# Conversion with four load tiles, three tiles for scale and low part, and a chunk begun two places after its load

## The chip, the cores and the metric

The kernel runs on one core of one Trainium2 chip. The metric is the time of one execution on the device in microseconds (us); the median of several executions is compared. The engines are TensorE (PE in the profile, its weight loads PEld), VectorE (DVE), ScalarE (ACT), GpSimd (POOL) and SyncE (SP), which here issues nearly all transfers. Each engine works through its own instructions in order.

## The reference

Two stages follow one another. The first is attention with heads mixed twice (8 batches, 12 heads, 448 tokens, 64 numbers per head), all in float32:

```
scores = scale * q @ k^T;  scores = einsum('bhij,hg->bgij', scores, w_pre)
attn = softmax(scores);    attn   = einsum('bhij,hg->bgij', attn, w_post)
attn_out = attn @ v
```

The second takes the result as 3584 tokens of 768 numbers:

```
h = x @ w_in;  g = h - tanh(h);  out = g @ w_out     # w_in 768 x 2048, w_out 2048 x 768
```

`w_in` and `w_out` arrive as float64, that is as pairs of 32-bit words. The kernel makes two float32r numbers of each, a high and a low part, whose sum carries the precision that the products need. This step is the conversion.

## The kernel before, in words

**The attention stage** goes through 180 places (`NPL`), the passes of the loop `for p in range(NPL + 3)`. A place handles two groups of 10 tokens with all 12 heads: `premix` (L521, TensorE mixes the heads of the scores `t`), `expo` (L530 maximum on DVE, L532 exponential on ACT), and for the place before `norm` (L541, L542 on DVE, L543 `wr` on POOL) and `mix` (L560 on TensorE, with `e` and `wr`), whose result ACT copies at the start of the next place (`at`, L570 or L577). Between them a place gets jobs by a planner: scores (L477, copies L482), preparation of k and q (L417, L443), values (L602, copy L620). TensorE's order in a place is premix, jobs, mix. A place is therefore short (about 3.8 us) with scores alone and longer (5 to 6 us) with values. The tile that `mix` writes exists once, so the next mix waits for the copy `at`.

**Gathers.** Each place first issues on SP two gathers `t<-s` (L510), for the premix two places later. Then `issue` sends up to 6 waiting transfers, first those of the attention (`queue`), then those of the conversion (`slow`), in order, and only those that were entered in an earlier place.

**The conversion** works in 56 chunks, 24 of `w_in` (128 x 512 numbers, the wide ones) and 32 of `w_out` (128 x 384, the narrow ones), in the order 6 wide, 8 narrow, and so on. `narrow_chunk` is a generator of eleven steps: L80 (DVE) makes `cm` from the load tile `cr`; L82 (ACT) and L83 (DVE); L85 (ACT); L87 (DVE) writes `cs`; L89 and L94 (DVE); L96 and L98 (POOL) make the sum in `cm`; L102 (ACT) writes the high part into `cs`; L104 (POOL) writes the low part into `cl`; the last step enters the transfers of `cs` and `cl` to DRAM. `narrow_steps` keeps up to two chunks active and lets them step in turn. It enters a load when a load tile is free, and begins a chunk when its load was issued at least one place earlier (`landed(1)`); that is a count of places and no wait. The wait for the data itself stands on DVE, at L80. When no chunk is active, a step passes with nothing done.

`Steps` spreads these steps evenly: from place 4 on, `conv.place()` runs 617/164 = 3.76 steps at the end of every place, after the mix was written down. At place 177 `conv.rest(now)` runs what is left; between its steps `now` issues all waiting transfers. Directly after that the first weights (`load_w(0)`, `w<-ws`) and the inputs of the second stage (`load_x`, `rx<-xs`) are issued on SP.

At the end `in_order` fixes the order of instructions on every engine as they were written down. A conversion step that has to wait therefore holds up what is written behind it on its engine: on POOL the next `wr`, on ACT the next `at`, on DVE the next `zs` and maximum.

**The second stage** computes h, the gate and the sum for 7 blocks of 512 tokens, with 16 slices of the weights each.

Of the kernel before, what the change touches and what calls it, by code (L numbers as in the profile page):

```python
# [11 lines left out]
F32R = mybir.dt.float32r  # L12
I32 = mybir.dt.int32
# [8 lines left out]
def raw(ap):  # L22

    return ap.bitcast(F32)
# [7 lines left out]
CW = 512  # L32
# [5 lines left out]
def narrow_steps(nc, pool, dma, chunks):  # L38

    def load(src):
        p, n2 = src.shape
        r = pool.tile([p, CW, 2], I32, name="cr", tag="cr", bufs=3)[:, : n2 // 2]
        return r, dma(r.rearrange("p n t -> p (n t)"), src)


    todo, loads, active = list(chunks), [], []  # L50
    yield
    while todo or loads or active:
        while todo and len(loads) + len(active) < 3:
            src, dst = todo.pop(0)
            loads.append((*load(src), dst))
        while loads and len(active) < 2:
            r, landed, dst = loads[0]
            if not landed(1):
                break
            loads.pop(0)  # L60
            active.append(narrow_chunk(nc, pool, dma, r, dst))
        for it in list(active):
            if next(it, "end") == "end":
                active.remove(it)
            else:
                yield
        if not active:
            yield


def narrow_chunk(nc, pool, dma, r, dst):
    p, n, _ = r.shape
    hi, lo = r[:, :, 1], r[:, :, 0]
    m = pool.tile([p, CW], F32, name="cm", tag="cm", bufs=2)[:, :n]
    s = pool.tile([p, CW], I32, name="cs", tag="cs", bufs=2)[:, :n]
    u, w = hi, lo


    lim = 122879.9921875
    nc.vector.tensor_scalar(m, hi.bitcast(F32), lim, -lim, op0=ALU.min, op1=ALU.max)  # L80
    yield "step"
    nc.scalar.mul(m, m, 2.0**-112)  # L82
    nc.vector.tensor_scalar(w, lo, 8, None, op0=ALU.logical_shift_right)  # L83
    yield "step"
    nc.scalar.mul(w.bitcast(F32), w, 2.0**-44)  # L85
    yield "step"
    nc.vector.tensor_scalar(s, hi, -(2**31), None, op0=ALU.bitwise_and)  # L87
    yield "step"
    nc.vector.scalar_tensor_tensor(  # L89
        out=u, in0=m.bitcast(I32), scalar=3, in1=s, op0=ALU.logical_shift_left, op1=ALU.bitwise_or  # L90
    )
    yield "step"

    nc.vector.tensor_scalar(s, u, -(2**23), None, op0=ALU.bitwise_and)  # L94
    yield "step"
    nc.gpsimd.tensor_tensor(out=m, in0=w.bitcast(F32), in1=s.bitcast(F32), op=ALU.mult)  # L96
    yield "step"
    nc.gpsimd.tensor_tensor(out=m, in0=m, in1=u.bitcast(F32), op=ALU.add)  # L98
    yield "step"
    fh = s.bitcast(F32R)  # L100
    fl = pool.tile([p, CW], F32R, name="cl", tag="cl", bufs=2)[:, :n]
    nc.scalar.copy(fh, m)  # L102
    yield "step"
    nc.gpsimd.tensor_sub(fl, m, raw(fh))  # L104
    yield "step"
    for to, part in zip(dst, (fh, fl)):
        if len(to.shape) == 3:
            part = part.rearrange("p (f n) -> p f n", f=to.shape[1])
        dma(to, raw(part))
    yield "step"  # L110
# [38 lines left out]
def kernel_body(  # L149
# [189 lines left out]
    with ExitStack() as st:  # L339
# [403 lines left out]
        scores_of(1, 0)  # L743
        NPL = NG // 2
        conv = Steps(narrow_steps(nc, cv, partial(dma, to=slow), chunks), 11 * len(chunks) + 1, NPL - 16)


# [200 lines left out]
```

## Time and profile before

| | us |
|---|---|
| median of 3 runs | 1794.49 (1794.04 to 1794.81) |
| the profiled execution | 1788.92 |
| its span, first to last instruction | 1787.2 |
| TensorE busy | 1751.0 |
| VectorE busy | 1128.3 |
| ScalarE busy | 1000.5 |
| GpSimd busy | 320.1 |

Busy times are sums over one engine's instructions and overlap between engines. The time that counts is the chain of work that ends last; idle time of an engine beside that chain costs nothing.

### The profile page before, as it was taken

How to read it: one execution, taken by the hardware profiler on the slowest of the kernel's cores; microseconds unless marked ns; L12 is line 12 of the kernel's file. 1: busy time of each engine (PE TensorE's matmuls, PEld its weight loads, DVE VectorE, ACT ScalarE, POOL GpSimd, SP SyncE). 2: the span in 40 equal slices, each digit the busy share in tenths (PEclk: the TensorE clock that was granted, in tenths of full speed). 3: DMA queues.
4: the chain of work that ended last, by engine and by line, in shares of the span. 5: the costliest groups of instructions: out<-in, count | busy, mean ns of one | idle time of the engine just before them, and what ended most of it. 6: DMA issues, size and time to landing. Idle time of an engine off the chain costs nothing.

```text
span 1787.2 us, 41382 instructions
## 1 busy us (share of the span) xinstructions
PE 1751.0 (98%) x16572; PEld 1425.6 (80%) x16572; DVE 1128.3 (63%) x2362; ACT 1000.5 (56%) x2051; POOL 320.1 (18%) x417
## 2 busy tenths in 40 slices
PE   8999999999999999999999999999999999999998
PEld 6777777777777777777888888888888888888887
DVE  5676777777777767664556566565565565655555
ACT  5777877777777776765343443433434434444333
POOL 1333333333333333321010010000000000000000
PEclk9999999999999999999999999999999999999999
DMA  8668687777967687565655655655656655655651
GB/s 176 204 196 216 194 236 224 217 215 215 249 203 218 215 213 220 178 202 216 255 207 194 248 193 207 241 193 214 229 197 216 224 208 204 228 217 190 230 194 36
DMA packets 232816, 372.32 MB, mean 208 GB/s; under 512 B 98992, under 2 KB 207536, under 8 KB 218288
## 3 DMA queue, kind: packets, MB, share of 16 engines
q1 hardware_dynamic: 231740, 368.45, 64.0%
q8 instruction: 131, 2.15, 0.5%
q10 hardware_dynamic: 884, 1.22, 0.2%
q14 instruction: 61, 0.50, 0.1%
HBM read 245.37 MB, written 47.19 MB: 164 GB/s over the span
## 4 chain that ended last, share of the span: by engine, by line
PE 87%; DMA 4%; ACT 4%; DVE 3%; issue 1%; POOL 0%; SPq 0%; ACTq 0%; DVEq 0%; POOLq 0%
PE ps_o L560 13%; PE ps_h L257 8%; PE ps_h L258 8%; PE ps_h L262 8%; PE ps_m L602 8%; PE ps_p L521 7%; PE ya L305 6%; PE ya L302 6%; PE ya L303 6%; PE ps_q L477 5%; PE yb L305 3%; PE yb L303 3%; PE yb L302 3%; DMA t<-s 2%; PE ps_m L443 1%
## 5 line engine op out<-in xcount | busy, mean ns | idle before, releaser
L560 PEld LDWEIGHTS ps_o<-wr,e 60*112 60x112 f32 (+1 forms) x5760 | 306.2, 176 | 44.3 <-POOL wr L543 21.8
L560 PE MATMUL ps_o<-wr,e 60*112 60x60 f32 (+1 forms) x5760 | 315.5, 259 | 14.3 <-POOL wr L543 7.7
L530 DVE TENSOR_REDUCE mx<-ps_p 128x1 f32<-128x448 f32 x360 | 207.7, 619 | 163.9 <-PE ps_p L521 163.7
L532 ACT ACTIVATE e<-ps_p,mx 128x448 f32<-128x448 f32 x360 | 225.7, 634 | 101.9 <-DVE mx L530 99.4
L289 ACT CAST gh<-r 128x512 fp32r<-128x512 f32 x112 | 69.6, 621 | 372.6 <-DVE r L282 372.6
L258 PE MATMUL ps_h<-xl,w 128*128 128x512 f32 x672 | 264.4, 393 | 0.0
L257 PE MATMUL ps_h<-xh,w 128*128 128x512 f32 x672 | 264.3, 393 | 0.0
L570 ACT COPY at<-ps_o 112x960 f32<-112x960 f32 x156 | 153.7, 985 | 93.8 <-PE ps_o L560 93.2
L247 POOL TENSOR_TENSOR xl<-rx,xh 128x512 fp32r<-128x512 f32 x38 | 55.6, 1464 | 731.2 <-ACT xh L246 731.2
L521 PE MATMUL ps_p<-t,wpre 60*64 60x448 f32 (+1 forms) x1440 | 180.8, 569 | 3.9 <-DMA t<-s 2.7
L305 PE MATMUL ya<-w,gl 128*128 128x512 f32 x448 | 177.0, 395 | 0.7 <-DVE gl L290 0.7
L278 DVE SCALAR_TENSOR_TENSOR r<-qa,ps_h 128x512 f32<-128x512 f32 x112 | 77.1, 688 | 159.2 <-ACT t L275 159.2
L302 PE MATMUL ya<-w,gh 128*128 128x512 f32 x448 | 174.8, 390 | 1.0 <-ACT gh L289 1.0
L303 PE MATMUL ya<-w,gh 128*128 128x512 f32 x448 | 174.8, 390 | 0.0
L602 PEld LDWEIGHTS ps_m<-at,vr 112*64 112x64 f32 x3072 | 147.5, 137 | 31.0 <-ACT at L577 10.9
L262 PE MATMUL ps_h<-xh,w 128*128 128x512 f32 x672 | 170.6, 389 | 0.0
L602 PE MATMUL ps_m<-at,vr 112*64 112x120 f32 (+1 forms) x3072 | 161.6, 261 | 8.4 <-ACT at L577 3.1
L272 ACT ACTIVATE u<-ps_h 128x512 f32<-128x512 f32 x112 | 67.0, 599 | 152.9 <-PE ps_h L262 152.9
L262 PEld LDWEIGHTS ps_h<-xh,w 128*128 128x128 f32 x672 | 126.3, 188 | 26.3
L258 PEld LDWEIGHTS ps_h<-xl,w 128*128 128x128 f32 x672 | 127.5, 190 | 23.7
L257 PEld LDWEIGHTS ps_h<-xh,w 128*128 128x128 f32 x672 | 127.4, 190 | 23.4
L543 POOL TENSOR_TENSOR wr<-wpost,zs 128x120 f32<-128x120 f32 x180 | 70.2, 390 | 402.9 <-DVE zs L542 293.6
(93 smaller groups left out, 3038.0 us busy)
## 6 DMA issues: line engine op xcount, KB each, us to landing
w<-ws SPq DMA_DIRECT2D x112, 1536.0 KB
t<-s SPq DMA_DIRECT2D x342, 210.0 KB
cr<-in_moe_w_in_dram SPq DMA_DIRECT2D x24, 512.0 KB
cr<-in_moe_w_out_dram SPq DMA_DIRECT2D x32, 384.0 KB
vr<-in_v_dram SPq DMA_DIRECT2D x24, 448.0 KB
kr<-in_k_dram SPq DMA_DIRECT2D x23, 448.0 KB
out_dram<-ob SPq DMA_DIRECT2D x24, 384.0 KB
qr<-in_q_dram SPq DMA_DIRECT2D x23, 360.0 KB
```

The lines of the kernel that those rows point to most:

```text
L257: nc.tensor.matmul(ph, wh[:, fs], xh, start=(c == 0), stop=False)
L258: nc.tensor.matmul(ph, wh[:, fs], xl, start=False, stop=False)
L262: nc.tensor.matmul(ph, wl[:, fs], xh, start=False, stop=(c == NK - 1))
L302: nc.tensor.matmul(y, gh[:, tok], wh[:, es], start=first, stop=False)
L303: nc.tensor.matmul(y, gh[:, tok], wl[:, es], start=False, stop=False)
L305: nc.tensor.matmul(y, gl[:, tok], wh[:, es], start=False, stop=last)
L521: nc.tensor.matmul(pss[r][halves[j], :], wpre[k, :], ts[j][k, :], start=True, stop=True)
L530: nc.vector.tensor_reduce(out=mx, in_=ps, axis=AX.X, op=ALU.max, negate=True)
L532: nc.scalar.activation(e, ps, AF.Exp, bias=mx, scale=1.0, accum_out=zs[:, 0, r : r + 1])
L560: nc.tensor.matmul(ps[:CP, j, c * GP : (c + 1) * GP].rearrange("p (h i) -> p h i", i=GI)[:, :, r * GH : (r + 1) * GH], e[k, c * CP : (c + ...
L570: nc.scalar.copy(ats[i0][:, :, :, at : at + 2 * GI].rearrange("p c h (j i) -> p j (c h) i", j=2), ps[:CP, :, : NC * GP].rearrange("p j (x ...
L602: nc.tensor.matmul(pv[j * D : (j + 1) * D, r, :n], vt[:, j, c, :], ats[i][:, c, 2 * hp + j, :n], start=(c == 0), stop=(c == NC - 1),)
```

## The change

Three tiles get one more buffer each: the load tile `cr` (4 for 3), `cs` and `cl` (3 for 2). Loads are entered as long as fewer than four chunks are loaded or active. A chunk begins when its load was issued at least two places earlier.

```diff
     def load(src):
         p, n2 = src.shape
-        r = pool.tile([p, CW, 2], I32, name="cr", tag="cr", bufs=3)[:, : n2 // 2]
+        r = pool.tile([p, CW, 2], I32, name="cr", tag="cr", bufs=4)[:, : n2 // 2]
...
-        while todo and len(loads) + len(active) < 3:
+        while todo and len(loads) + len(active) < 4:
             src, dst = todo.pop(0)
             loads.append((*load(src), dst))
         while loads and len(active) < 2:
             r, landed, dst = loads[0]
-            if not landed(1):
+            if not landed(2):
                 break
...
-    s = pool.tile([p, CW], I32, name="cs", tag="cs", bufs=2)[:, :n]
+    s = pool.tile([p, CW], I32, name="cs", tag="cs", bufs=3)[:, :n]
...
-    fl = pool.tile([p, CW], F32R, name="cl", tag="cl", bufs=2)[:, :n]
+    fl = pool.tile([p, CW], F32R, name="cl", tag="cl", bufs=3)[:, :n]
```

## Rows read from the trace of the kernel before

**Rows 1.** The page: span, and busy time of each engine

```profile
span 1787.2 us, 41382 instructions
...
PE 1751.0 (98%) x16572; PEld 1425.6 (80%) x16572; DVE 1128.3 (63%) x2362; ACT 1000.5 (56%) x2051; POOL 320.1 (18%) x417
```

**Rows 2.** Stretches: us, busy and count of PE, PEld, DVE, ACT, POOL; clock, DMA, GB/s

```profile
40.00:840.00 800.00, 776.48 (x11434) 601.81 (x11432) 562.15 (x1519) 593.48 (x1352) 256.10 (x346) 0.99 0.73 212
...
108.00:114.00 6.00, 6.00 (x69) 4.34 (x66) 3.27 (x9) 4.30 (x10) 1.62 (x2) 0.72 0.54 195
722.00:730.00 8.00, 8.00 (x93) 5.64 (x93) 4.22 (x14) 5.51 (x13) 3.43 (x5) 0.79 0.54 185
794.00:806.00 12.00, 10.74 (x114) 7.87 (x116) 5.37 (x15) 6.53 (x16) 3.90 (x6) 0.72 0.29 107
...
870.00:1700.00 830.00, 829.32 (x4200) 703.64 (x4199) 486.56 (x700) 343.97 (x585) 52.92 (x36) 1.00 0.60 217
```

**Rows 3.** Waits of TensorE, 40 to 840 us: us in total, times, longest

```profile
PE ps_o L560 <- POOL wr L543: 6.5, 9, 1.3
PE ps_o L560 <- ACT at L570: 5.7, 8, 1.5
PE ps_m L602 <- ACT at L577: 3.1, 5, 1.0
PE ps_m L602 <- ACT at L570: 2.7, 4, 1.8
PE ps_m L602 <- DMA vr<-in_v_dram: 2.4, 2, 1.4
PE ps_p L521 <- DMA t<-s: 1.1, 2, 0.8
```

**Rows 4.** Waits of VectorE for the conversion's transfers, 40 to 840 us

```profile
DVE cs L87 <- DMA ws<-cs: 6.9, 3, 3.5
...
DVE cm L80 <- DMA cr<-in_moe_w_in_dram: 3.4, 4, 1.0
...
DVE cm L80 <- DMA cr<-in_moe_w_out_dram: 1.6, 2, 1.2
```

**Rows 5.** Timeline around the first two chunks: start, us, engine, line, idle before

```profile
51.86 0.43 DVE L80 TENSOR_SCALAR cm<-cr 128x512 f32<-128x512 f32 x1 [0.90 <-DMA cr<-in_moe_w_in_dram]
...
55.28 2.68 PE L602 MATMUL ps_m<-at,vr 112*64 112x120 f32 x48 [1.82 <-ACT at L570]
...
73.16 1.15 ACT L102 CAST cs<-cm 128x512 fp32r<-128x512 f32 x2
73.87 1.28 POOL L104 TENSOR_TENSOR cl<-cm,cs 128x512 fp32r<-128x512 f32 x1 [2.74 <-ACT cs L102]
...
75.45 1.27 POOL L104 TENSOR_TENSOR cl<-cm,cs 128x512 fp32r<-128x512 f32 x1
...
75.54 1.78 PE L560 MATMUL ps_o<-wr,e 60*112 60x60 f32 x32 [0.52 <-POOL wr L543]
...
80.57 1.53 SPq L369 DMA_DIRECT2D cr<-in_moe_w_in_dram  x2
```

**Rows 6.** Timeline of two later gaps

```profile
104.38 1.45 DVE L83 TENSOR_SCALAR cr<-cr 128x512 int32<-128x512 int32 x1
...
107.52 1.78 PE L560 MATMUL ps_o<-wr,e 60*112 60x60 f32 x32 [1.50 <-ACT at L570]
...
795.26 3.00 PE L560 MATMUL ps_o<-wr,e 60*112 60x60 f32 x32 [1.26 <-POOL wr L543]
```

**Rows 7.** Durations: min/median/max ns with starts; busy us, mean ns, idle before

```profile
L521 PE MATMUL ps_p<-t,wpre x1440: 536/587/1005, 26.4 to 838.7; 60*64 60x448 f32 x172, 48*64 48x448 f32 x8
...
L83 DVE TENSOR_SCALAR cr<-cr x56: 350/420/1547, 53.6 to 783.0; 128x384 int32<-128x384 int32 x32, 128x512 int32<-128x512 int32 x24
...
L104 POOL TENSOR_TENSOR cl<-cm,cs 128x384 fp32r<-128x384 f32 x32 | 32.1, 1003 | 55.1 <-ACT cs L102 54.9
...
L104 POOL TENSOR_TENSOR cl<-cm,cs 128x512 fp32r<-128x512 f32 x24 | 30.7, 1278 | 35.0 <-ACT cs L102 35.0
```

**Rows 8.** Timeline at the end of the attention stage

```profile
827.28 0.49 SPq L334 DMA_DIRECT2D w<-ws  x1
829.42 8.07 SPq L238 DMA_DIRECT2D rx<-xs  x12
...
836.00 0.61 ACT L246 CAST xh<-rx 128x512 fp32r<-128x512 f32 x1
```

## The prediction

> **What bounds the kernel now.** I read the page's busy line first, then the table of stretches, then who waits for whom, then the timeline. TensorE works for 98% of the span [rows 1]. In the stretch from 870 to 1700 us it is busy 829.3 of 830 us at a granted clock of 1.00 [rows 2]: that stage is full, and the change does not reach it. The attention stage, where the conversion runs, has TensorE busy 776.5 of 800 us: 23.5 us idle. In three stretches of that stage the granted clock falls to the lower of its two levels (1.2 instead of 2.4 GHz) for a while: 6 x 0.28, 8 x 0.21 and 12 x 0.28 us, 6.7 us together [rows 2]. In the timeline the first follows a gap of 1.50 us, the last a gap of 1.26 us [rows 6]. So at most 23.5 + 6.7 = 30 us can be gained at all, 1.7% of the time.
>
> Of the idle time, TensorE waits 6.5 us for `wr` on POOL, 5.7 + 3.1 + 2.7 us for a copy on ACT, and 2.4 + 1.1 us for a DMA [rows 3]. `wr` and the copies stand in order on engines which the conversion shares, so its steps matter less by their length than by what they stand in front of.
>
> **Part 1: the waits that the change names.** DVE waits 6.9 us in 3 places for an output of `cs` to leave its buffer, and 3.4 + 1.6 us in 6 places for a load [rows 4]. Of these twelve microseconds only the first loads reach TensorE. Just before 51.86 DVE waits 0.90 us for the first chunk and then again for the second; the copies behind them are late, and TensorE stands idle 1.82 us before 55.28 [rows 5]. With two places of 4.5 us (180 premixes from 26.4 to 838.7 us, 812/179) [rows 7] the load has landed. I take -1.8 us. The ends are 0, if DVE meets something else there, and -11.9, if every such wait counted; the others lie beside TensorE's own work and I value them at nothing.
>
> **Part 2: the order of the steps, the larger part.** I followed the loop of `narrow_steps` by hand, 617/164 = 3.76 steps a place. Before, two chunks begin together, and the third load alone is ready when they end; the fourth and fifth are issued only then, side by side at 80.57 [rows 5]. From then on the two active chunks are half a chunk apart, and now and then one runs alone. After the change four loads are issued at once. Chunks 0 and 1 begin together one place later, end in the same round, and 2 and 3 are there to begin in the same round. Every pair does so: the conversion runs in lockstep to its end, two equal steps behind one another. Each pair ends with one step in which nothing is active, 28 of them, and 10 stand at the start. That is 1 + 616 + 38 = 655 steps against 654 that 174 places run, so the conversion lasts until place 177 instead of 170.
>
> The price of a pair in lockstep is in the trace, since the first pair ran so. ACT converts both `fh` at 73.16, POOL makes the first `cl` at 73.87, and `wr` comes behind it, so that TensorE waits 0.52 us before 75.54; the second `cl` follows at 75.45 [rows 5]. For the narrow chunks, where one such POOL operation takes 1003 instead of 1278 ns [rows 7], 0.28 less: 0.24 us. There are 12 wide and 16 narrow pairs: 12 x 0.52 + 16 x 0.24 = 10.1 us. Three things come on top, counted in the order of the steps:
> - In about five places both `cl` stand ahead of the next `wr`, and the place behind is a short one: 5 x 1.1 (between 1.00 and 1.28) = 5.5 us.
> - In five places four POOL steps stand in a row, two of them ahead of a short place: 4 x 1.3 = 5.2 us of POOL in a place of 3.3 us gives 1.9, the narrow one 0.3: 2.2 us.
> - Nine short places hold three or four ACT steps, against five now; four more at 0.5 us (the mean ACT gap: (5.7 + 3.1 + 2.7)/17 = 0.68, less what a long neighbour hides) = 2.0 us.
>
> Together 19.8 us. What they replace is all of the four POOL and ACT rows but the 1.82 us of part 1: 18.0 - 1.8 = 16.2 us [rows 3]. In them are gaps of a kind that lockstep ends. At 104.38 DVE's L83 takes 1.45 us, where the shortest takes 0.35, while POOL is busy with the other chunk; the copy behind it is late and TensorE waits 1.50 us. At 795.26 one chunk alone runs its last steps close together, and TensorE waits 1.26 us [rows 6, 7]. Part 2 is +3.6 us in gaps. Against it I set one of the clock's falls, the last, whose cause (a chunk alone) cannot recur: half of its 12 x 0.28, -1.7 us. So +1.9 us. The ends: 10.1 us in place of 16.2 and no fall of the clock, -12.8; every pair with both `cl` ahead of `wr`, 12 x 1.80 + 16 x 1.24 = 41.4, of which the long places hide some four tenths, leaves 25: +9.
>
> A rule of the Trainium skill bears on the L83 row. "SBUF — State Buffer", section "Who interferes with whom", says that a VectorE operation in its two-port modes and a GpSimd operation take a pair of ports as an exclusive lock, and the later one blocks until the other has ended. The row agrees: 350 to 1547 ns for the same operation. By the rule lockstep should pay, since one chunk's DVE steps no longer lie beside the other's POOL steps; what that would give is the first rival below.
>
> **Part 3: transfers come in bursts.** The bytes are the same, but a wide pair now sends 2 loads of 512 KB and 4 outputs of 256 KB within two places, 2 MB, where before they came one chunk at a time. The stage moves 212 GB/s at a DMA share of 0.73 [rows 2], so a place of 4.5 us could carry 212/0.73 x 4.5 = 1.3 MB, of which two gathers take 0.42. A burst takes two places and a bit, and is over before the next, 6.1 places later. It costs something only where loads of `v` or `k` fall into it, about five times. TensorE now loses 2.4 + 1.1 us in 4 waits for a DMA [rows 3], 0.9 us each. I take one more of them, +0.9 us, between 0 and 5 x 0.9 = 4.5, because a gather has two places to land in. An output also makes SP wait for the second `cl` of its pair, and the gathers stand behind it on SP; they are issued two places ahead, which hides that.
>
> **Part 4: the end of the stage.** Places 171 to 177 had no conversion and now carry the last pair; some of them have no scores, so that little lies between premix and mix and a late `wr` is not covered. I take +1.0 us: two such places at 0.5, the gap of the first pair; between 0 and 4. The last four outputs are issued ahead of `w` at 827.28 and of the x loads at 829.42 [rows 8], because one step is left for the rest. They wait for the last `cl`, that is for two narrow ones, 2 x 1.00 us [rows 7]. SP then issues `rx` about 2 us later, and ACT asks for the first of them at 836.00 [rows 8]. I hold that for hidden, 0, and keep 4 us as its price if it is not. The third tile for `cs` and `cl` and the shift of the addresses cost nothing by themselves.
>
> **Sum.** -1.8 + 1.9 + 0.9 + 1.0 = +2.0 us on the profiled execution of 1788.92 us, whose span is 1787.2 [rows 1]: 1790.9 us. The median of the runs is 1794.49, 5.6 us above the profiled one, so 1796.5 us. The first term is the surest; the second is a difference of two counts and may have either sign. Less than 0.2%, 3.6 us, cannot be told from no change here.
>
> **Rivals.**
> 1. Faster: lockstep ends the collisions and the runs of one chunk alone, and its own price stays at that of the first pair. Gaps 16.2 to 10.1, two of three falls of the clock gone (-3.4), part 1 -1.8, parts 3 and 4 +1.9: -9.4; with half the gaps and one fall of the clock less -4.6. Taken as -7: 1787.5. For it speak the gaps of 1.50 and 1.26 [rows 6]; against it, that the three later steps on POOL now double up.
> 2. Slower: POOL becomes the engine that TensorE waits for. Where two `cl` (2.0 to 2.6 us) or four POOL steps (4.1 to 5.2) stand ahead of `wr`, each pair costs over 1 us. Part 2 at its upper end, +9, parts 3 and 4 +1.9, part 1 -1.8: +9, 1803.5. It decides from the point where `wr` comes more than about half a microsecond later than now in most pairs. For it: the 0.52 us gap with only one `cl` ahead [rows 5]; against it: POOL has 544 us of 800 free in the stage [rows 2].
> 3. Slower at the end: the x loads land late and ACT stands at 836.00 in front of the copy that the mix needs: +4 on the sum, 1800.5.
>
> **How the numbers follow.** No measurable change 0.38; rival 1 0.29; rival 2 0.26; rival 3 0.07. So faster by over 0.2% 0.29, within 0.38, slower 0.33. The range of 1786 to 1804 us holds the forecast and rival 3, about two thirds of rival 1 (down to -8.5) and over half of rival 2 (up to +9.5); the forecast's own range is 1791 to 1798.
>
> **What will show it.** The two `cm` (L80) of each pair one behind the other, from first to last, and the last `cl` just ahead of the `w` load, at about 830 us: if the chunks are staggered, part 2 is wrong from the root. No wait of DVE for `cr` and none for `cs`. The wait of TensorE before the values at about 55 us gone. POOL's row among TensorE's waits up from 6.5 to 10 or more, ACT's rows down, DMA's about 5. L83 close to 0.35 and 0.42 us. If POOL's row stays under 7 and the clock falls once at most, rival 1 holds; if it passes 16, rival 2.

## The result and the profile after

The changed kernel takes 1800.96 us (median of 6 runs, 1797.02 to 1806.81), the kernel before on the same chip 1793.82 us (6 runs, 1789.32 to 1794.81). The ratio is 1.0048 [1.0028, 1.0069] (in brackets, here and below, the interval that holds it with 95%). It is the figure on record and not the quotient of the two medians, which is 1.0040. By the medians the kernel is 7 us slower, where 2 us were forecast. The profiled execution took 1797.02 us, 8.1 more than that of before.

The page of the changed kernel:

```profile
span 1795.3 us, 41327 instructions
...
PE 1750.4 (98%) x16572; PEld 1426.7 (79%) x16572; DVE 1105.3 (62%) x2362; ACT 999.6 (56%) x2051; POOL 314.8 (18%) x417
```

TensorE does the same work in the same busy time; VectorE is even busy 23.0 us less than before [rows 1]. So in this pair of executions the loss is idle time of TensorE, and the table of stretches says where. The first row is of the kernel before, the others of the changed one (start and end, us, then busy and count of PE, PEld, DVE, ACT, POOL, granted clock, DMA share, GB/s):

```profile
840.00:844.75 4.75, 3.59 (x58) 3.38 (x56) 2.79 (x7) 4.75 (x10) 0.74 (x2) 0.85 1.00 417
...
40.00:848.70 808.70, 776.38 (x11438) 602.37 (x11438) 540.24 (x1520) 593.47 (x1354) 252.08 (x346) 0.99 0.71 209
848.70:853.45 4.75, 3.58 (x43) 3.37 (x39) 2.21 (x5) 3.56 (x6) 1.57 (x2) 0.53 0.98 353
870.00:1700.00 830.00, 829.64 (x4204) 704.70 (x4204) 486.15 (x700) 344.66 (x586) 51.67 (x36) 1.00 0.61 219
```

At 844.75 us before and at 853.45 us after, TensorE begins the second stage. So the same work, from 40 us to the end of the attention stage, takes 804.75 us before and 813.45 us after, 8.7 us more. TensorE is busy for 776.48 + 3.59 = 780.07 us of it before [rows 2] and for 776.38 + 3.58 = 779.96 us after, and idle for 24.7 and 33.5 us. The second stage is as full as it was. The waits of TensorE in this stretch of the changed kernel are (us in total, times, longest):

```profile
PE ps_o L560 <- POOL wr L543: 12.6, 12, 2.8
PE ps_o L560 <- ACT at L570: 7.3, 9, 1.4
PE ps_p L521 <- DMA t<-s: 5.4, 4, 2.1
PE ps_m L602 <- DMA vr<-in_v_dram: 3.5, 3, 1.3
PE ps_m L602 <- ACT at L577: 2.4, 5, 0.7
PE ps_p L521 <- ACT at L570: 1.1, 1, 1.1
PE ps_m L602 <- ACT at L570: 0.6, 2, 0.3
```

[Rows 3] end at 840 us, just ahead of the last mix, and don't show every row. Up to the end of the stage these of the kernel before belong in the comparison as well:

```profile
PE ps_o L560 <- POOL wr L543: 7.7, 10, 1.3
...
PE ps_p L521 <- ACT at L570: 1.0, 1, 1.0
PE ps_o L560 <- POOL cl L104: 0.3, 1, 0.3
```

So `wr` rose from 7.7 to 12.6 us (+4.9) and DMA from 3.5 to 8.9 (+5.4). The copies on ACT went from 12.5 to 11.4 (-1.1), and `cl` from 0.3 to nothing.

**The waits that the change removes** are gone. Of DVE's waits on the conversion's transfers this one is left, against 6.9, 3.4 and 1.6 us [rows 4]:

```profile
DVE cm L80 <- DMA cr<-in_moe_w_in_dram: 0.4, 1, 0.4
```

The lines of L83 also lost their long ends (minimum, median, maximum in ns; 350, 420, 1547 before [rows 7]):

```profile
L83 DVE TENSOR_SCALAR cr<-cr x56: 349/368/437, 54.3 to 821.4; 128x384 int32<-128x384 int32 x32, 128x512 int32<-128x512 int32 x24
```

**Lockstep.** In VectorE's timeline (start, us, engine, line) the first operation of a chunk now comes in twos to the end:

```profile
113.50 0.75 DVE L80 TENSOR_SCALAR cm<-cr 128x512 f32<-128x512 f32 x2
...
818.64 0.61 DVE L80 TENSOR_SCALAR cm<-cr 128x384 f32<-128x384 f32 x2
```

In 21 of the 28 pairs the two L80 stand directly behind one another; before, only those of the first pair did.

**The longest new gap**, in the timeline (last bracket: idle time before, and its releaser):

```profile
727.07 0.17 DVE L542 RECIPROCAL zs<-zs 128x2 f32<-128x2 f32 x1
...
727.50 1.16 ACT L102 CAST cs<-cm 128x512 fp32r<-128x512 f32 x2
728.22 2.49 POOL L104 TENSOR_TENSOR cl<-cm,cs 128x512 fp32r<-128x512 f32 x2 [4.30 <-ACT cs L102]
...
730.67 0.50 POOL L543 TENSOR_TENSOR wr<-wpost,zs 128x120 f32<-128x120 f32 x1
...
731.23 1.78 PE L560 MATMUL ps_o<-wr,e 60*112 60x60 f32 x32 [2.75 <-POOL wr L543]
```

The reciprocals are there at 727.24. POOL stood idle 4.30 us for ACT, then makes both low parts, 2.49 us, and `wr` comes behind them. Another gap has the same name and another cause:

```profile
514.57 1.28 DVE L89 SCALAR_TENSOR_TENSOR cr<-cm,cs 128x512 int32<-128x512 int32 x2
...
515.77 0.75 DVE L94 TENSOR_SCALAR cs<-cr 128x512 int32<-128x512 int32 x2
...
516.44 0.20 DVE L541 TENSOR_SCALAR zs<-zs 128x1 f32<-128x1 f32 x2
...
517.02 0.39 POOL L543 TENSOR_TENSOR wr<-wpost,zs 128x120 f32<-128x120 f32 x1 [4.66 <-DVE zs L542]
...
517.46 1.78 PE L560 MATMUL ps_o<-wr,e 60*112 60x60 f32 x32 [1.12 <-POOL wr L543]
```

Here POOL is free and waits itself. The late one is `zs` on DVE, behind two L89 and two L94. The row "POOL wr" names the last step of a chain, not the engine that was held up.

**The start.** The wait before 55.28 [rows 5] is gone, and a longer one stands four microseconds later:

```profile
46.27 2.63 SPq L369 DMA_DIRECT2D cr<-in_moe_w_in_dram  x4
...
49.00 5.70 SPq L510 DMA_DIRECT2D t<-s  x6
...
59.26 0.98 PE L521 MATMUL ps_p<-t,wpre 60*64 60x448 f32 x8 [2.08 <-DMA t<-s]
```

A premix waits for a gather that was issued behind four loads of 512 KB; before, three loads went out together.

**The end.** Both last low parts stand just ahead of the first weight load, and ACT now waits for `rx`:

```profile
834.93 1.96 POOL L104 TENSOR_TENSOR cl<-cm,cs 128x384 fp32r<-128x384 f32 x2
...
837.32 0.45 SPq L334 DMA_DIRECT2D w<-ws  x1
...
845.07 0.62 ACT L246 CAST xh<-rx 128x512 fp32r<-128x512 f32 x1 [2.14 <-DMA rx<-xs]
...
847.32 1.78 PE L560 MATMUL ps_o<-wr,e 60*112 60x60 f32 x32 [1.28 <-POOL wr L543]
...
850.27 3.24 PE L560 MATMUL ps_o<-wr,e 60*112 60x60 f32 x32 [1.17 <-ACT at L570]
```

### The profile page after: what moved, and what is told of

Same layout as the page of the kernel before. It is cut to its first block, busy times and chain, and to the rows that moved or that the text cites. A ratio compares the mean times of both kernels' runs of the same rounds, so it can differ in the third digit from the quotient of the medians.

```text
span 1795.3 us, 41327 instructions
## 1 busy us (share of the span) xinstructions
PE 1750.4 (98%) x16572; PEld 1426.7 (79%) x16572; DVE 1105.3 (62%) x2362; ACT 999.6 (56%) x2051; POOL 314.8 (18%) x417
## 3 DMA queue, kind: packets, MB, share of 16 engines
q10 hardware_dynamic: 884, 1.22, 0.2%
## 4 chain that ended last, share of the span: by engine, by line
PE 85%; DMA 4%; ACT 4%; DVE 3%; issue 2%; POOL 1%; SPq 1%; ACTq 0%; POOLq 0%; DVEq 0%
PE ps_o L560 12%; PE ps_h L258 8%; PE ps_h L257 8%; PE ps_h L262 8%; PE ps_m L602 8%; PE ps_p L521 7%; PE ya L305 6%; PE ya L302 6%; PE ya L303 6%; PE ps_q L477 5%; PE yb L305 3%; PE yb L303 3%; PE yb L302 3%; DMA t<-s 3%; ACT e L532 1%
## 5 line engine op out<-in xcount | busy, mean ns | idle before, releaser
L560 PEld LDWEIGHTS ps_o<-wr,e 60*112 60x112 f32 (+1 forms) x5760 | 307.1, 176 | 51.2 <-POOL wr L543 27.4
L560 PE MATMUL ps_o<-wr,e 60*112 60x60 f32 (+1 forms) x5760 | 316.7, 260 | 20.6 <-POOL wr L543 12.6
L521 PE MATMUL ps_p<-t,wpre 60*64 60x448 f32 (+1 forms) x1440 | 179.1, 567 | 8.2 <-DMA t<-s 7.0
L543 POOL TENSOR_TENSOR wr<-wpost,zs 128x120 f32<-128x120 f32 x180 | 69.9, 388 | 502.4 <-DVE zs L542 411.0
```

Source lines behind the costliest of these rows:

```text
L521: nc.tensor.matmul(pss[r][halves[j], :], wpre[k, :], ts[j][k, :], start=True, stop=True)
L560: nc.tensor.matmul(ps[:CP, j, c * GP : (c + 1) * GP].rearrange("p (h i) -> p h i", i=GI)[:, :, r * GH : (r + 1) * GH], e[k, c * CP : (c + ...
```

## The experiments

My theory: the order of the steps (lockstep) makes the loss. Its rivals: the bursts of transfers, the late end of the conversion, the first fill of four loads, the tiles themselves. A time is the median of 12 runs where nothing else is said. All ratios are to the kernel before, run on the same chip beside them (medians 1794.51, 1791.93 and 1793.79 us in the three groups). Where an edit adds lines, the profile's numbers are one or two higher (L544 and L561 are L543 and L560).

**1. Changed kernel, second chunk begun half a chunk behind the first**

```diff
-        while loads and len(active) < 2:
+        while loads and len(active) < 2 and (not active or active[-1][1] >= 5):
...
+            it[1] += 1     # steps that this chunk has made
```

> The changed kernel with one thing undone: the second chunk begins only when the first has done five of its eleven steps, so the chunks run half a chunk apart with the same four load tiles, three tiles for scale and low part and two places of distance. Theory (the order of the steps costs): TensorE's wait for wr falls from 12.6 us to 6 or less, the two low parts never stand ahead of one wr, the conversion ends at place 171, and the time is at or below the kernel before, 1785 to 1794 us. Rival (more loads and outputs in flight, or the moved addresses, cost by themselves): it stays with the changed kernel at 1798 to 1802 us.

1793.63 us, ratio 1.0002 [0.9979, 1.0026]. No two L80 stand together any more, and the first of TensorE's waits reads

```profile
PE ps_o L561 <- POOL wr L544: 7.6, 9, 2.1
```

The row of `wr` is not at 6 or less, but it is where the kernel before has it (7.7). The tiles, the later begin and the shift of the addresses are all still there; the order of the steps differs, and the loss is gone. With the order, the times at which transfers leave and the place where the conversion ends differ too; numbers 6 and 9 take these up.

**2. Kernel before with four load tiles alone** (two output tiles, one place)

```diff
-name="cr", tag="cr", bufs=3)
+name="cr", tag="cr", bufs=4)
...
-        while todo and len(loads) + len(active) < 3:
+        while todo and len(loads) + len(active) < 4:
```

> The kernel before with four load tiles and nothing else: by the loop this alone puts the chunks in lockstep (34 idle steps), begun one place behind the load's issue, with two tiles for scale and low part. Theory (lockstep costs): slower like the changed kernel, 1798 to 1804 us, with TensorE's wait for wr at 10 us or more, and the waits of VectorE for the load at 52 us back. Rival (three output tiles or the later begin cost): within 0.2% of the kernel before.

1810.02 us (6 runs), 1.0086 [1.0058, 1.0114]. The fourth load alone brings the lockstep (21 of 28 pairs with L80 back to back) and a loss of the same order: the ratio is above 1.0048, but the two intervals overlap. But the loss doesn't lie where I expected it:

```profile
PE ps_o L560 <- POOL wr L543: 8.8, 10, 2.6
PE ps_m L602 <- DMA vr<-in_v_dram: 7.6, 4, 4.1
...
PE ps_p L521 <- DMA t<-s: 5.1, 5, 2.5
```

`wr` stayed under 10, the waits for a DMA rose to 12.7 us, and DVE still waits 6.7 us for `cs`. The profiled execution was the slowest of the six (1818.92 us). Which of these the loss hangs on here was not tried.

**3. Kernel before with three output tiles alone** (`cs` and `cl` with `bufs=3`)

> The kernel before with three tiles for scale and low part and nothing else; the order of the steps is that of the kernel before. Theory: the 6.9 us that VectorE waits for outputs go, little of it lies on TensorE's path, so 0 to 2 us faster, not to be told from no change. Rival (moved addresses or deeper outputs cost): 3 us slower or more.

1791.9 us, 0.9989 [0.9968, 1.0011]. DVE's wait for `cs` is gone, no L80 stand together after the first pair, and no change of the time shows. The interval ends at 0.9968, 5.7 us, so the 6.9 us of that wait were not worth their full length.

**4. Changed kernel, steps denser, so that the conversion ends nine places sooner**

```diff
-11 * len(chunks) + 1, NPL - 16
+11 * len(chunks) + 39, NPL - 16
```

> The changed kernel with the steps per place raised from 3.76 to 3.99, so that the conversion, still in lockstep, ends at place 168 instead of 177. Theory (the late end costs about 1 to 4 us, the pairs in the middle the rest): 1 to 4 us faster than the changed kernel, still slower than the one before. Rival (the late end is the whole loss): as fast as the kernel before. Second rival (denser steps cost more than the end gives back): slower than the changed kernel.

1805.34 us, 1.0052 [1.0034, 1.007]. No gain shows from an earlier end. The denser steps put the pairs at other places (`wr` 10.9 us, DMA 14.3 us), so this alone doesn't acquit the end; number 9 adds to it.

**5. Changed kernel, at most two transfers of the conversion per place**

```diff
-            for x in (queue, slow):
-                while x and most and x[0][0] < place[0]:
+            for x, n in ((queue, most), (slow, 2)):
+                while x and n and x[0][0] < place[0]:
```

> The changed kernel with at most two of the conversion's transfers issued per place instead of up to six. By the loop the order of the steps on every compute engine stays that of the changed kernel; only SP sends the loads and outputs of a pair over three places. Theory (bursts make up the larger part of the loss, the doubled POOL steps the smaller): TensorE's waits for t and vr fall from 8.9 us to 5 or less, those for wr stay at 10 to 13, the time falls by 3 to 6 us to 1795 to 1798. Rival (the POOL steps alone are the loss): no gain, 1799 to 1803 us.

1803.7 us (9 runs), 1.0051 [1.003, 1.0073]. By then I held the bursts for the larger part, because DMA's waits had risen as much as `wr`. No gain showed, and the waits that should have fallen stayed: DMA is 8.6 us for 8.9, so how the transfers are grouped doesn't make them. The two intervals still leave room for a gain of up to about 5 us; number 6 says more on the bursts. `wr` is 12.4 us in 12 waits, and the longest gap stands in the same place of the program:

```profile
732.11 2.49 POOL L104 TENSOR_TENSOR cl<-cm,cs 128x512 fp32r<-128x512 f32 x2 [4.30 <-ACT cs L102]
...
735.11 1.13 PE L560 MATMUL ps_o<-wr,e 60*112 60x60 f32 x18 [2.75 <-POOL wr L543]
```

**6. Changed kernel, second chunk two steps behind the first** (as number 1, with 2 for 5)

> The changed kernel with the second chunk begun when the first has done two steps: the low parts of a pair never fall into one place any more, but the pair's loads and outputs still leave within about one place. Theory (POOL and bursts each hold a part): TensorE's wait for wr at 8 us or less, waits for DMA still at 6 us or more, 1793 to 1798 us. If POOL is the whole loss: like the kernel with half a chunk of distance, 1794 us or less. If bursts are the whole loss: 1799 us or more.

1793.61 us, 1.0002 [0.9985, 1.0019]. A lag of two steps suffices, though the pairs still send their transfers close together:

```profile
PE ps_p L522 <- DMA t<-s: 6.2, 4, 2.7
PE ps_o L561 <- POOL wr L544: 6.1, 6, 2.3
...
PE ps_m L603 <- DMA vr<-in_v_dram: 1.1, 3, 0.5
```

DMA's waits are 7.3 us, nearer to the changed kernel's 8.9 than to 3.5; `wr` is below its 7.7 of before. The time fits both the 1793 to 1798 us and the 1794 us or less of the expectation.

**7. Changed kernel, two loads in the first fill instead of four**

```diff
-        while todo and len(loads) + len(active) < 4:
+        while todo and len(loads) + len(active) < most:    # most: 2, and 4 once the first chunk begins
```

> The changed kernel with two loads at the start instead of four; the other two are issued when the first chunks have begun, and the lockstep stays. Theory: the wait of 2.08 us for the gather before 59.26 us goes, and perhaps the fall of the clock right behind it (3.4 us at half speed), 2 to 4 us faster than the changed kernel. Rival: the wait only moves to the later two loads, no change.

1802.29 us, 1.0057 [1.0035, 1.0079]. The gap of 2.08 us at 59 us is gone, and no gain shows; one of 2 us could not be told from none in this spread. `wr` is 12.6 us in 12 waits, as in the changed kernel.

**8. Numbers 1, 5 and 7 together; and once more (12)**

> Half a chunk of distance, two loads at the start and at most two of the conversion's transfers per place, on the changed kernel's tiles. Theory: TensorE's waits for DMA at 4 us or less, for wr at 7, and 3 to 6 us faster than the kernel before: 1788 to 1791. Rival (with the chunks apart the order of the steps decides, and gaps only move): within 0.2% of the kernel before.

1789.32 us, 0.9979 [0.9963, 0.9996]. The same kernel again:

> Half a chunk of distance, two loads at the start and at most two transfers per place, once more, since its interval reached almost to no change: 0.1 to 0.4% faster than the kernel before if the first result holds; within 0.1% if it was chance.

1790.33 us, 0.9989 [0.9969, 1.0009]. The two say 0.1 to 0.2% under the kernel before, and the second is not clear of no change. They also show how well a single profile repeats. The row of `wr` came out the same in both, 7.6 us in 9 waits, the longest 2.1. The row of `t<-s` was 2.3 us in 2 waits in the first and 4.3 us in 4 in the second.

**9. Number 6 with fewer steps per place, so that the conversion ends within a place of the changed kernel's** (`11 * len(chunks) - 20`, place 176)

> Two steps of distance as before, and the steps per place lowered from 3.76 to 3.64, so that the conversion ends at place 176, as late as the changed kernel's to one place. Theory (the doubled POOL steps of a lockstep pair are the loss, not the late end): as the kernel with two steps of distance, 1791 to 1796 us. Rival (the late end is the loss): 1799 us or more, like the changed kernel.

1787.56 us, 0.9979 [0.996, 0.9997]. No loss shows from a late end if the chunks are apart. In lockstep, number 4 saw no gain from an earlier one.

**10. Changed kernel, the low part of every pair's second chunk made by VectorE**

```diff
-    nc.gpsimd.tensor_sub(fl, m, raw(fh))
+    (nc.vector if odd else nc.gpsimd).tensor_sub(fl, m, raw(fh))
```

> The changed kernel, still in lockstep with its late end, but the low part of the second chunk of a pair is made by VectorE instead of GpSimd, so two of them never stand ahead of one wr. Theory (doubled POOL steps): TensorE's wait for wr falls from 12.6 us to 8 or less, the gap of 2.75 us near 731 us to 1.5 or less, and the time to 1793 to 1798 us. Rival (other costs of lockstep: doubled ACT and DVE steps, the late end): 1800 us or more, and the time lost for wr comes back as waits behind ACT or VectorE.

1802.97 us (8 runs), 1.0075 [1.0048, 1.0103]. My theory here, that the doubled POOL steps alone make `wr` late, fell. The row stays at 12.0 us in 11 waits. The place of the longest gap shows why:

```profile
731.95 1.16 ACT L102 CAST cs<-cm 128x512 fp32r<-128x512 f32 x2
732.67 1.27 POOL L104 TENSOR_TENSOR cl<-cm,cs 128x512 fp32r<-128x512 f32 x1 [4.32 <-ACT cs L102]
...
733.14 1.34 DVE L104 TENSOR_TENSOR cl<-cm,cs 128x512 fp32r<-128x512 f32 x1 [1.79 <-ACT cs L102]
734.40 0.20 DVE L541 TENSOR_SCALAR zs<-zs 128x1 f32<-128x1 f32 x2
...
734.95 0.39 POOL L543 TENSOR_TENSOR wr<-wpost,zs 128x120 f32<-128x120 f32 x1 [1.01 <-DVE zs L542]
...
735.39 0.80 PE L560 MATMUL ps_o<-wr,e 60*112 60x60 f32 x12 [2.48 <-POOL wr L543]
```

The moved step now waits on DVE 1.79 us for ACT's second copy and stands ahead of `zs`. POOL is free, and `wr` is as late as before.

**11. Number 8 with every low part on VectorE**

> Half a chunk of distance, two loads at the start, two transfers per place, and all low parts made by VectorE. If POOL's step in front of wr is still the largest single cost: wait for wr at 5 us or less, 1784 to 1788 us. Rival (VectorE, which is busier, then holds up the maxima and wr's input): 1789 us or more.

1797.46 us, 1.0025 [1.0008, 1.0043], with `wr` at 10.5 us. No chunks are in lockstep here, yet `wr` is late and the kernel a little slower. That fits a late `wr` costing time by another way too, but doesn't show it: TensorE is idle 26.9 us, where number 8's two profiles have 23.1 and 25.2, and the median granted clock of the runs was lower as well, 0.9895 for 0.993.

Side by side, from 40 us to the first matmul of the second stage in the profiled execution, in us. "Idle" is the length of this stretch less the time that TensorE is busy in it; `wr` and DMA are the waits in it:

| kernel | L80 back to back | idle | `wr` | DMA | ratio |
|---|---|---|---|---|---|
| kernel before | first pair only | 24.7 | 7.7 | 3.5 | 1 |
| 6 two steps apart | no | 23.5 | 6.1 | 7.3 | 1.0002 |
| 9 two apart, late end | no | 25.5 | 7.3 | 8.4 | 0.9979 |
| 1 half a chunk apart | no | 25.5 | 7.6 | 7.0 | 1.0002 |
| 8 and 12 all three | no | 23.1, 25.2 | 7.6 | 5.0, 6.5 | 0.9979, 0.9989 |
| 3 outputs only | first pair only | 26.7 | 7.7 | 6.5 | 0.9989 |
| 11 low parts on VectorE | no | 26.9 | 10.5 | 4.4 | 1.0025 |
| changed kernel | yes | 33.5 | 12.6 | 8.9 | 1.0048 |
| 5 two transfers | yes | 31.2 | 12.4 | 8.6 | 1.0051 |
| 7 two loads first | yes | 31.5 | 12.6 | 6.3 | 1.0057 |
| 10 second low part moved | yes | 33.2 | 12.0 | 8.7 | 1.0075 |
| 4 sooner end | yes | 35.5 | 10.9 | 14.3 | 1.0052 |
| 2 four loads only | yes | 35.6 | 8.8 | 12.7 | 1.0086 |

Every kernel with lockstep is 0.5 to 0.9% slower, and none without it is beyond 0.25%. TensorE's idle time tells the two groups apart without exception: 31.2 to 35.6 us with lockstep, 23.1 to 26.9 without. No single row of waits does that. From the changed kernel down to number 10 `wr` is at 12.0 to 12.6 us, but in the last two rows it is lower and much of the loss shows itself as waits for a DMA.

## Why the prediction was right or wrong

**What bounds it: right.** The second stage is untouched, and in the two profiles all that changed is idle time of TensorE in the attention stage.

**Part 1 (-1.8): the waits went, the gain didn't come.** DVE's twelve microseconds of waiting shrank to 0.4 and the gap of 1.82 us went. One of 2.08 us took its place, a gather behind four loads. The prediction left out the first fill: part 3 counted the bursts of later pairs only. In number 3 the wait for `cs` goes and no gain shows; in number 7 the new gap is gone and the time doesn't fall.

**Part 2: the mechanism and the direction were right, the size only in sum.** Lockstep from first to last pair, L83 at 349 to 437 ns and POOL's row above 10 came as forecast. Over the same work the rows of POOL and ACT together rose from 20.5 to 24.0 us, that is +3.5, where parts 1, 2 and 4 had -1.8 + 3.6 + 1.0 = +2.8 in gaps. Some of this nearness is luck. The 18.0 us that the count replaced lacked the row of 1.0 (L521 behind `at`), `cl` with 0.3 and the wait of 1.16 us for `wr` before 842.40. And the price came from the first pair and from POOL and ACT alone: the two L89 and two L94 ahead of `zs` on DVE were not counted, nor that POOL stands idle for ACT's second copy before it begins. The gap of 1.50 us before 107.52, which the prediction laid to the collision on L83 and held to be ended by lockstep, is still 1.22 us at the same mix (108.61); there the copy stands behind both L102 on ACT.

The 1.7 us set against part 2 for a fall of the clock didn't come. TensorE is busy for the same time within 0.1 us, and the clock fell four times for three before. Over the runs the clock speaks against the forecast as well. Its median was 0.989 in the six runs of the changed kernel and 0.987 to 0.990 in the other kernels with lockstep. In the 92 runs of the kernel before that stood beside the experiments it was 0.991 to 0.992, and in the kernels with the chunks apart 0.9895 to 0.9935. An estimate from all recorded runs, each kernel's against one another: a run is 1.7 us longer where its mean granted clock is lower by 0.001. By that some 3 us of the medians' difference come with a lower clock. Whether the gaps cause it was not tried.

**What was mis-sized.** In the two profiles TensorE's idle time rose by 8.8 us and the forecast was 2.0 in all. The measured 1800.96 us lies inside the range of 1786 to 1804 but outside the forecast's own 1791 to 1798; slower by over 0.2% had been given 0.33. The largest part of the difference is the wait for a DMA, +5.4 for +0.9 (part 3). The fall of the clock that didn't go is 1.7, and the last places are +2.5 for +1.0 (part 4). The other gaps on POOL and ACT, parts 1 and 2, came to +1.0 for +1.8. The kernel before has only one profile, though, and a row of a DMA varies. Against the kernels on the same tiles with the chunks apart (1, 6 and 9), the changed kernel has 8 to 10 us more idle time: 5.0 to 6.5 us of it are `wr`, 1.7 to 2.2 ACT and 0.5 to 1.9 a DMA. That is what lockstep costs, and most of it stands in the row that part 2 named.

**The first rival fell.** The collisions on L83 ended, as the rule in "SBUF — State Buffer", "Who interferes with whom" of the Trainium skill lets one expect of steps that no longer lie beside one another, and DVE is busy 23 us less. The kernel is slower all the same. Most of the time that DVE saved lay beside TensorE's work; what counts is what stands ahead of `zs` and `wr`.

**Part 3 (+0.9): the row rose further, and doesn't decide.** DMA's waits rose by 5.4 us in the profile. But a smaller first fill (7: 6.3 us) brought no gain that shows, and kernels with the chunks apart hold nearly as long waits (9: 8.4 us) at no loss. Number 3, with the order of the kernel before, has 6.5 us at no loss, where the kernel before has 3.5. Spreading the transfers (5) left the row at 8.6 us and so tells nothing of its worth. Numbers 2 and 4, with 12.7 and 14.3 us, are a warning that this doesn't hold for every order of steps.

**Part 4 (+1.0): there, larger, and not the cause.** The last pair ended just ahead of the weights' load, as forecast. From 819 us before and 825 us after, the gaps up to the second stage add up to 1.7 and 4.2 us, +2.5. The third rival came in part: ACT waits 2.14 us for `rx` at 845.07. But number 9, which ends one place earlier, is not slower than before.

**The second rival** had the size nearly right (1803.5 us), and its mark of 16 us on `wr` was not reached. Its mechanism holds with a correction: it is not POOL alone that becomes the engine waited for. The pair of equal steps holds up whichever in-order engine stands on the way to `wr` (POOL at 728, DVE at 515, DVE again in number 10).

**Open:** how the 7 us divide among the three engines, since number 10 moved the gap instead of removing it; whether four loads alone (2) cost more than the whole change, and why their loss stands in other rows.

## What to carry to other kernels

Another buffer in front of two interleaved streams of steps can put them into the same rhythm; see by hand when the second one begins, and keep them some steps apart (a condition on the first one's steps did it here: 1.0048 to 1.0002). A removed wait counts only if the engine that sets the end waited for it too. Where engines work in order, price a doubled step by what stands behind it on every engine of the chain to the critical instruction, and read a row's releaser as the last link of that chain only.

## What the runs showed of the hardware

- The granted clock fell behind gaps of TensorE: in the changed kernel behind those of 2.08, 2.13 and 2.75 us, to the lower of its two levels for a while (columns as above):

```profile
60.00:64.00 4.00, 4.00 (x36) 3.53 (x34) 2.99 (x8) 2.96 (x8) 0.02 (x1) 0.57 0.47 152
...
579.00:583.00 4.00, 4.00 (x38) 3.65 (x36) 2.69 (x7) 3.02 (x8) 0.42 (x2) 0.57 0.73 199
732.00:737.00 5.00, 5.00 (x50) 3.27 (x46) 1.81 (x4) 2.48 (x6) 0.00 (x0) 0.66 0.98 276
```

  A fourth fall came behind a gap of only 1.25 us before 522.81 (0.59 from 524 to 528 us), which followed one of 1.12 us before 517.46. In the kernel before, the falls came behind gaps of 1.50, 1.01 and 1.26 us, and none behind its longest, the 1.82 us before 55.28 (1.00 from 55 to 62 us). So the length of a gap alone doesn't tell whether the clock falls. The link was seen, not tested: number 7 has no gap and no fall at 60 us, and is not faster.
- One kernel's executions spread by more than the effect: number 1 took 1784.3 to 1805.3 us in 12 runs, at mean granted clocks of 0.996 in the shortest and 0.986 in the longest. A difference of 7 us needs many runs of each.
- A VectorE operation beside a POOL operation was still longer in lockstep, in one place at least: at 729.61 us L80 took 1.31 us beside the two low parts, where its median is 0.36 us.
